# Second chunk of rows through the DMA transposes, six tiles of w1 on the first chunk, scales one by one

## The chip, the cores and the metric

The kernel runs on one core of one Trainium2 chip. The metric is the device time of one execution in microseconds (us), lower is better; a program's time is the median of its runs.

## The reference, cut to what matters

```python
def reference(A_x, A_w_r, A_w_i, B_w1, B_w2):      # x: (1, 2048, 1024), w1: (1024, 3584), w2: (3584, 1024)
    xn = layernorm(A_x)                            # over the last axis, eps 1e-5
    X = rfft2(xn) * (A_w_r + 1j * A_w_i)
    s = irfft2(X)
    g = silu(silu(xn @ B_w1) @ B_w2)
    return A_x + s * g
```

Everything is float32. The two matrix products are the bulk of the arithmetic; the 2-D Fourier filter `s` is made of matrix products with constant matrices and of butterflies.

## The kernel before, in words

The 2048 rows are four chunks `c` of 512 rows, each of four blocks `p` of 128 rows. The 3584 hidden columns are 28 tiles `f` of 128. To keep float32 accuracy every factor is split into two float16 halves, a high one and a low one, and a product takes three passes (high·high, high·low, low·high).

**The first product.** `mm1(c, f)` makes one tile (c, f): 24 matmuls 128x128 by 128x512 into one PSUM tile `pa`. It needs `xnT[c]`, the normalised chunk transposed (both halves, all four blocks), and `w1t[f]`, both halves of w1's tile f. The matmuls are on TensorE (PE in the profile). Which tile follows which is the list `order` in the main loop. After a tile, ScalarE (ACT) evacuates it with a Silu (`evac`, L465) into `h32`. The `pa` tiles and the column sums share four PSUM buffers in rotation.

**w1's tiles.** `weights1` loads a tile `w1r` by the SP queue, takes the maximum of each partition on VectorE (`maxi`, DVE L274), sums it over the partitions with a small matmul (`column_sums`, PE L258), makes a power-of-two scale from that (`scales`, four to six tiny DVE operations, L279 to L287), then the high half on ACT (`split`, L251) and the low half on DVE (`rest`, L254). In the kernel before, scales are made for two tiles at once. Raw tiles and finished tiles share seven buffers.

**Chunks.** `ln_gen(c)` normalises a chunk: `stats` on DVE (two BN_STATS and an aggregate per block), three tiny POOL operations for the scale and shift, the normalisation itself on ACT (`norm`, L700). Chunks 0 and 1 are then transposed on PE (`trans`, eight 128x128 transposes a block), and their halves are taken from PSUM (`hi` on ACT L713, `lo` on DVE L717). Chunks 2 and 3 are in `TURNED`: `turned` normalises into a tile `xp` whose columns are permuted, takes the halves in SBUF (`xs`; high on ACT L678, low on DVE L671), and has the SP queue issue two DMA transposes a block (`turn`, L664). `xp` has two buffers, so the third block's normalisation waits until the first block's low half is done. `xs` has one buffer for all chunks, and it is also the buffer of the Fourier stage's `V`.

**What follows a pair of tiles.** When tiles f and f+1 of chunks 0 and 1 (or 2 and 3) are evacuated, `hidden(q, g)` turns them into seven products' operands: `hr` and a rewrite of `h` on DVE (L494, L495, L499), then `hosum` (from `hr`) and `hoone` (from `h`): a high half on ACT (L251), a low half on DVE (L254), and three or four stores by SP (L488). `hosum` and `hoone` have one buffer each: the next pair's high half waits until the stores of the pair before have landed. `h32` has two buffers.

**What sets the order.** Each engine runs its instructions in the order in which the program issues them and waits at each for its semaphores. The main loop issues a tile of PE work, then steps the generators in the queues `wq` (weights) and `bg` (chunks, then the Fourier stages); for the first four tiles the numbers of steps are written out by hand, later `work` steps them by two counters of issued work. Once built, the order on every engine is fixed. `fa_mat(c, p)` is a block's first Fourier matmuls (24 small ones, L773 to L775), `fa_evac` its two copies on ACT (L782, L783); `FILL` places the first two of chunk 0 between tiles.

Of the kernel before, what the change touches and what calls it, by code (L numbers as in the profile page):

```python
# [23 lines left out]
IORDER = (1, 3, 0, 2)  # L24
SUMMED = (4, 5)
TURNED = (2, 3)
FILL = ((1, 0), (3, 0))
EXTRA = (4, 5, 6, 7, 20, 22, 24)

# [98 lines left out]
def spectral_ffn(ctx, tc, x, w_r, w_i, w1, w2, ca, kc, ci, tw, pm, out):  # L128
# [132 lines left out]
    def weights1():  # L261

        raw = {}

        def load(i):
            raw[i] = fp.tile([128, 8, 128], F32, name=f"w1r{i}", tag="w1", bufs=7)  # L270
            nc.sync.dma_start(raw[i], w1v[:, :, i * 128:(i + 1) * 128])

        def maxi(i):
            nc.vector.tensor_reduce(m1[:, i:i + 1], raw[i], axis=AX.XY, op=OP.max, apply_absolute_value=True)  # L274

        def scales(i, k):
            sl = slice(i, i + k)
            ps = column_sums(f"s1_{i}", m1[:, sl], k)
            nc.vector.tensor_single_scalar(e1[:, sl].bitcast(I32), ps.bitcast(I32), 0x7F800000, op=OP.bitwise_and)  # L279
            nc.vector.tensor_single_scalar(e1[:, sl], e1[:, sl], 2.0**-100, op=OP.max)  # L280
            nc.vector.reciprocal(r1[:, sl], e1[:, sl])
            nc.vector.tensor_single_scalar(rs[:, sl], r1[:, sl], 2.0**14, op=OP.mult)
            nc.gpsimd.tensor_single_scalar(s1[:, sl], e1[:, sl], 2.0**-24, op=OP.mult)
            if (i + k) % 2 == 0:
                p = (i + k) // 2 - 1
                nc.vector.tensor_tensor(ep[:, p:p + 1], e1[:, 2 * p:2 * p + 1], e1[:, 2 * p + 1:2 * p + 2], op=OP.max)
                nc.vector.tensor_tensor(hs[:, p:p + 1], r1[:, 2 * p:2 * p + 1], r1[:, 2 * p + 1:2 * p + 2], op=OP.min)  # L287
                nc.gpsimd.tensor_single_scalar(hs[:, p:p + 1], hs[:, p:p + 1], 2.0**7, op=OP.mult)

        new = {}  # L290

        def split(i):
            new[i] = fp.tile([128, 2, 8, 128], F16, name=f"w1_{i}", tag="w1", bufs=7)
            high(new[i][:, 0], raw[i], rs[:, i:i + 1])

        def rest(i):
            w1t[i] = w = new.pop(i)
            low(w[:, 1], raw.pop(i), rs[:, i:i + 1], w[:, 0])

        for i in range(4):  # L300
            load(i)
        yield 0
        maxi(0)
        yield 0
        maxi(1)
        yield 0
        scales(0, 2)
        yield 0
        split(0)
        yield 0  # L310
        rest(0)
        yield 0
        split(1)
        rest(1)
        maxi(2)
        maxi(3)
        yield 0
        scales(2, 2)
        split(2)
        rest(2)  # L320
        yield 2
        split(3)
        rest(3)
        yield 2
        def ahead(i):

            if i < NFT and i not in raw and i - len(used1) <= 4:
                load(i)
                load(i + 1)

        last = None
        for i in range(4, NFT, 2):
            while i not in raw:
                ahead(i)
                yield 0
                if last is not None:
                    rest(last)
                    last = None
            maxi(i)
            if last is not None:  # L340
                rest(last)
            yield 0
            maxi(i + 1)
            yield 0
# [12 lines left out]
            yield 0.2  # L357
            last = i + 1
        rest(last)
# [89 lines left out]
    def mm1(c, f):  # L449
        ps = pf.tile([128, 512], F32, name=f"pa{c}_{f}", tag="ff")  # L450
        w, xt = w1t[f], xnT[c]
        terms = [(d, wh, xh) for wh, xh in ((0, 0), (0, 1), (1, 0)) for d in range(8)]
        if c + f:
            terms.sort(key=lambda k: k[0])
        for n, (d, wh, xh) in enumerate(terms):
            nc.tensor.matmul(ps, w[:, wh, d], xt[:, xh, d], start=(n == 0), stop=(n == 23))  # L456
        if c == 3:
            used1.add(f)
        q, g = f // 2, c // 2

        def evac():
            if (q, g) not in h32:
                h32[q, g] = H["p"].tile([128, 4, 512], F32, name=f"h32_{q}_{g}", tag="h32", bufs=2)
            hq = h32[q, g]
            nc.scalar.activation(hq[:, 2 * (c % 2) + f % 2], ps, AF.Silu, scale=s1[:, f:f + 1])  # L465
            if c % 2 and f % 2:
                return hidden(q, g)

        return evac
# [187 lines left out]
    def turned(c, stats, norm):  # L657
# [9 lines left out]
        for i in range(4):  # L667
# [15 lines left out]
                    stats(p)  # L683
            yield 2.5

    def ln_gen(c):
        ap = A["p"]

        def stats(p):
            xt = A["x"][c, p]  # L690
            st = ap.tile([128, 2, 6], F32, name=f"st{c}_{p}", tag="st", bufs=4)
            nc.vector.bn_stats(st[:, 0], xt[:, 0:512])
            nc.vector.bn_stats(st[:, 1], xt[:, 512:1024])
            mv = ap.tile([128, 2], F32, name=f"mv{c}_{p}", tag="mv", bufs=4)
            nc.vector.bn_aggr(mv, st.rearrange("p a b -> p (a b)"))
            v = ap.tile([128, 3], F32, name=f"v{c}_{p}", tag="v", bufs=4)
            nc.gpsimd.tensor_scalar(v[:, 0:1], mv[:, 1:2], EPS, 2.0**-20, op0=OP.add, op1=OP.mult)
            nc.gpsimd.tensor_tensor(v[:, 1:2], v[:, 0:1], mhalf, op=OP.pow)
            nc.gpsimd.tensor_scalar(v[:, 2:3], mv[:, 0:1], v[:, 1:2], -1.0, op0=OP.mult, op1=OP.mult)
            norm[p] = lambda o=xt, i=xt: nc.scalar.activation(o, i, AF.Identity, scale=v[:, 1:2], bias=v[:, 2:3])  # L700

        pst, norm = {}, {}

        def trans(p):
            ps = pt.tile([128, 8, 128], F32, name=f"tp{c}_{p}", tag="ft")
            xt = A["x"].pop((c, p))
            xv = xt.rearrange("s (d0 d1) -> s d1 d0", d1=8)
            for d in range(8):
                nc.tensor.transpose(ps[:, d], xv[:, d], ident)
            pst[p] = ps  # L710

        def hi(p):
            nc.scalar.activation(xnT[c][:, 0, :, p * 128:(p + 1) * 128], pst[p], AF.Copy)  # L713

        def lo(p):
            sl = slice(p * 128, (p + 1) * 128)
            nc.vector.tensor_tensor(xnT[c][:, 1, :, sl], pst.pop(p), xnT[c][:, 0, :, sl], op=OP.subtract)  # L717

        new_xnT(c)
        if c == 0:  # L720
            for p in range(2):
                stats(p)
                norm[p]()
            trans(0)
            hi(0)
            stats(2)
            norm[2]()
            trans(1)
            hi(1)
# [12 lines left out]
            lo(3)  # L742
            yield 0
            return
        if c in TURNED:
            yield from turned(c, stats, norm)
            return
        for i in range(4):
            pair = range(2 * (i % 2), 2 * (i % 2) + 2)
            for p in pair:  # L750
                if i < 2:
                    stats(p)
                else:
                    trans(p)
                    if c < 3:
                        load_x(c + 1, p)
            if i < 2:
                yield 2.5
                for p in pair:
                    norm[p]()  # L760
                continue
            for fn in (hi, lo):
                for p in pair:
                    fn(p)
            yield 2.5

    psa, l0 = {}, {}

# [641 lines left out]
    with tc.manual_schedule():  # L1410
# [70 lines left out]
        for c in range(4):  # L1481
            add(bg, fd_gen(c))

        order = [(c, f) for fs in ((0, 1, 2, 3), (4, 5)) for c in range(2) for f in fs]
        order += [(2, 0), (2, 1), (2, 2), (3, 0), (3, 1), (2, 3), (3, 2), (3, 3), (2, 4), (2, 5), (3, 4), (3, 5)]
        order += [(c, f + i) for f in range(6, NFT - LAST, 2) for c in range(4) for i in range(2)]
        order += [(2 * g + c, f + i) for g in range(2) for f in range(NFT - LAST, NFT, 2) for c in range(2) for i in range(2)]
# [2 lines left out]
        for n, (c, f) in enumerate(order):  # L1490
# [32 lines left out]
            if left == 0:  # L1523
                for j, k in ((2, 0), (2, 1), (3, 0)):
                    load_h(0, j, k, nc.sync)
            if n < 4:
                slot(wq)
                for _ in range((2, 0, 1, 1)[f]):
                    slot(bg)
                settle()  # L1530
                fresh_ev[0] = ev
                tick()
                continue
# [81 lines left out]
```

## Time and profile before

| | us |
|---|---|
| median of 3 runs (1239.05 to 1243.32) | 1241.05 |
| the profiled execution's own time | 1238.48 |
| its span (first to last instruction) | 1236.6 |
| PE busy, of the span | 1221.4 |
| DVE busy | 998.6 |
| ACT busy | 467.3 |
| DMA, mean | 237 GB/s |

PE, DVE, ACT and POOL are the four compute engines, PEld is PE's weight load, SP the engine that issues most transfers ("SPq" in the timeline is its queue). In a timeline a row has the start in us, the duration, the engine, the line and the operation, the tiles (out<-in) and, in brackets, the idle time before it and what ended that. Rows merge equal instructions that follow each other ("x24").

### The profile page before, as it was taken

How to read it: one execution, taken by the hardware profiler on the slowest of the kernel's cores; microseconds unless marked ns; L12 is line 12 of the kernel's file. 1: busy time of each engine (PE TensorE's matmuls, PEld its weight loads, DVE VectorE, ACT ScalarE, POOL GpSimd, SP SyncE). 2: the span in 40 equal slices, each digit the busy share in tenths (PEclk: the TensorE clock that was granted, in tenths of full speed). 3: DMA queues.
4: the chain of work that ended last, by engine and by line, in shares of the span. 5: the costliest groups of instructions: out<-in, count | busy, mean ns of one | idle time of the engine just before them, and what ended most of it. 6: DMA issues, size and time to landing. Idle time of an engine off the chain costs nothing.

```text
span 1236.6 us, 19106 instructions
## 1 busy us (share of the span) xinstructions
PE 1221.4 (99%) x7033; PEld 624.6 (51%) x7033; DVE 998.6 (81%) x1970; ACT 467.3 (38%) x614; POOL 117.3 (9%) x245
## 2 busy tenths in 40 slices
PE   8999999999999999999999999999999999999997
PEld 5545445444544454445445555554455555555544
DVE  7687988899798898886959899985196678798885
ACT  4865344333454565344533222122032222342212
POOL 2330000001000000010001121114111110000000
PEclk9999999999999999999999999999999999999999
DMA  8487476655768898759899999987979999997677
GB/s 251 136 171 186 134 224 204 186 147 166 218 178 237 283 280 242 213 178 272 206 287 223 281 256 200 303 251 238 294 206 275 293 287 320 319 348 292 223 261 231
DMA packets 271102, 293.67 MB, mean 237 GB/s; under 512 B 40096, under 2 KB 198816, under 8 KB 270624
## 3 DMA queue, kind: packets, MB, share of 16 engines
q1 hardware_dynamic: 250992, 233.66, 65.4%
q10 hardware_dynamic: 15984, 51.45, 12.0%
q0 software_dynamic: 4032, 7.34, 3.4%
q8 instruction: 55, 0.90, 0.3%
q14 instruction: 39, 0.32, 0.1%
HBM read 185.95 MB, written 102.25 MB: 233 GB/s over the span
## 4 chain that ended last, share of the span: by engine, by line
PE 87%; DMA 6%; DVE 4%; ACT 1%; issue 1%; SPq 0%; POOL 0%; ACTq 0%; DVEq 0%; POOLq 0%
PE pa L456 45%; PE pb L534 11%; PE pb L536 11%; PE pb L535 11%; DMA out_dram<-pl 2%; PE fx L945 2%; PE id L1285 1%; DMA sd<-s 1%; PE fx L947 1%; PE iu L1195 1%; PE fx L946 1%; ACT xp L700 1%; PE iu L1203 1%; DMA pl<-pd 1%; DMA fs<-sd 1%
## 5 line engine op out<-in xcount | busy, mean ns | idle before, releaser
L456 PE MATMUL pa<-xnT,w 128*128 128x512 f16 x2688 | 585.2, 379 | 1.1 <-ACT w L251 0.7
L456 PEld LDWEIGHTS <-w 128*128 128x128 f16 x2688 | 261.7, 98 | 312.1 <-DVE w L254 1.3
L534 PE MATMUL pb<-w,ht 128*128 128x512 f16 (+2 forms) x812 | 300.6, 372 | 0.0
L535 PE MATMUL pb<-w,ht 128*128 128x512 f16 (+2 forms) x812 | 300.6, 372 | 0.0
L536 PE MATMUL pb<-w,ht 128*128 128x512 f16 (+2 forms) x812 | 300.6, 372 | 0.0
L536 PEld LDWEIGHTS <-ht 128*128 128x128 f16 x812 | 79.3, 98 | 91.2
L534 PEld LDWEIGHTS <-ht 128*128 128x128 f16 x812 | 79.4, 98 | 86.8
L535 PEld LDWEIGHTS <-ht 128*128 128x128 f16 x812 | 79.3, 98 | 86.8
L465 ACT ACTIVATE h<-pa,s 128x512 f32<-128x512 f32 x112 | 75.5, 678 | 120.9 <-PE pa L456 108.9
L251 ACT ACTIVATE w<-jr,sc 128x512 f16<-128x512 f32 x98 | 68.1, 713 | 78.3 <-DMA jr<-in_B_w_dram 39.4
L254 DVE SCALAR_TENSOR_TENSOR hoone<-h,hs,hoone 128x2048 f16<-128x2048 f32 x28 | 65.7, 2345 | 8.9 <-ACT hoone L251 8.9
L254 DVE SCALAR_TENSOR_TENSOR w<-jr,sc,w 128x512 f16<-128x512 f32 x98 | 71.0, 743 | 2.1 <-ACT w L251 2.1
L251 ACT ACTIVATE hoone<-h,hs 128x2048 f16<-128x2048 f32 x28 | 56.0, 1998 | 38.5 <-DVE h L499 25.1
L251 ACT ACTIVATE hosum<-hr,hs 128x1536 f16<-128x1536 f32 x28 | 44.1, 1574 | 65.2 <-DVE hr L495 31.7
L972 ACT ACTIVATE zq<-Z,zs 128x1024 f16<-128x1024 f32 x16 | 18.4, 1149 | 107.6 <-DVE Z L1046 60.8
L254 DVE SCALAR_TENSOR_TENSOR hosum<-hr,hs,hosum 128x1536 f16<-128x1536 f32 x28 | 50.7, 1812 | 3.8 <-ACT hosum L251 3.8
L494 DVE TENSOR_TENSOR hr<-h 128x1024 f32<-128x1024 f32 x28 | 34.2, 1221 | 23.2 <-ACT h L465 23.1
L251 ACT ACTIVATE w<-w1r,rs 128x1024 f16<-128x1024 f32 x28 | 32.0, 1145 | 46.6 <-DVE w L254 31.4
L274 DVE TENSOR_REDUCE m<-w1r 128x1 f32<-128x1024 f32 x28 | 33.8, 1211 | 17.9 <-DMA w1r<-in_B_w_dram 17.9
L622 ACT ACTIVATE pl<-pl,c 128x512 f32<-128x512 f32 (+2 forms) x28 | 17.6, 657 | 72.3 <-DVE pl L601 33.9
L945 PE MATMUL fx<-vq,kq 128*128 128x256 f16 x192 | 43.2, 273 | 0.0
L946 PE MATMUL fx<-vq,kq 128*128 128x128 f16 x192 | 42.1, 219 | 0.0
(219 smaller groups left out, 1526.2 us busy)
## 6 DMA issues: line engine op xcount, KB each, us to landing
w1r<-in_B_w_dram SPq DMA_DIRECT2D x28, 512.0 KB, 6.3
hd_sum<-hosum SPq DMA_DIRECT2D x56, 256.0 KB, 2.9
hd_one<-hoone SPq DMA_DIRECT2D x56, 256.0 KB, 3.6
hd_dif<-hoone SPq DMA_DIRECT2D x56, 256.0 KB, 3.2
w2m<-in_B_w_dram SPq DMA_DIRECT2D x28, 512.0 KB, 5.2
ht<-hd_dif ACTq DMA_DIRECT2D x32, 448.0 KB, 6.0
jr<-in_B_w_dram SPq DMA_DIRECT2D x56, 256.0 KB, 6.8
ht<-hd_sum ACTq DMA_DIRECT2D x32, 448.0 KB, 5.5
```

What stands on the lines that cost most here:

```text
L251: nc.scalar.activation(hi, raw, AF.Copy, scale=scale)
L254: nc.vector.scalar_tensor_tensor(lo, raw, scale, hi, op0=OP.mult, op1=OP.subtract)
L274: nc.vector.tensor_reduce(m1[:, i:i + 1], raw[i], axis=AX.XY, op=OP.max, apply_absolute_value=True)
L456: nc.tensor.matmul(ps, w[:, wh, d], xt[:, xh, d], start=(n == 0), stop=(n == 23))
L465: nc.scalar.activation(hq[:, 2 * (c % 2) + f % 2], ps, AF.Silu, scale=s1[:, f:f + 1])
L494: tt(sums[:, 0:2], hq[:, 0::2], hq[:, 1::2], op=OP.subtract)
L534: nc.tensor.matmul(ps, hh[:, 0], w[:, 0], start=first, stop=False)
L535: nc.tensor.matmul(ps, hh[:, 0], w[:, 1], start=False, stop=False)
L536: nc.tensor.matmul(ps, hh[:, 1], w[:, 0], start=False, stop=last)
L945: nc.tensor.matmul(o, k[:, c, kh, 1], v[:, c, vh], start=(n == 0), stop=False)
L946: nc.tensor.matmul(ps[:, c, 0], k[:, c, kh, 2], v[:, c, vh, 128:256], start=False, stop=False)
L972: nc.scalar.activation(zqs[q][:, 0, :, 16 * j:16 * j + 16], zs_[u], AF.Copy, scale=zs)
```

## The change

Chunk 1 no longer takes the path over PE: it goes through a new generator `entering`, which normalises, splits and DMA-transposes block by block. So that PE has work meanwhile, the list `order` begins with the six tiles (0,0) to (0,5), then (1,0) to (1,5), where it was (0,0) to (0,3), (1,0) to (1,3), (0,4), (0,5), (1,4), (1,5). For that, tiles 4 and 5 of w1 are loaded and split early, and the scales of tiles 2 to 5 are made one by one, each column sum between two tiles. The string `ENTRY` gives the generators' steps behind the first five tiles ("b" a step of the chunks, "w" a step of the weights). Chunk 0's results of tiles 4 and 5 go to a spare tile `h32_early` and are copied into `h32` later. `FILL` puts chunk 0's first two Fourier blocks ahead of (0,4) and (1,0).

```diff
-FILL = ((1, 0), (3, 0))
-EXTRA = (4, 5, 6, 7, 20, 22, 24)
+FILL = ((0, 4), (1, 0))
+EXTRA = (20, 22, 24)
+ENTRY = ("bwbw", "bwbwb", "wbwbw", "wbwbw", "b")
...
     # weights1
         split(1)
+        yield 0
         rest(1)
+        load(4)
         maxi(2)
+        yield 0
+        scales(2, 1)
+        split(2)
+        load(5)
         maxi(3)
-        yield 0
-        scales(2, 2)
-        split(2)
         rest(2)
-        yield 2
+        yield 0
+        scales(3, 1)
+        maxi(4)
         split(3)
+        yield 0
         rest(3)
-        yield 2
+        yield 0
+        scales(4, 1)
+        yield 0
+        split(4)
+        yield 0
+        rest(4)
+        maxi(5)
+        yield 0
+        scales(5, 1)
+        yield 0
+        split(5)
+        yield 0
+        rest(5)
+        yield 0
...
-        for i in range(4, NFT, 2):
+        for i in range(6, NFT, 2):
...
     # mm1
-        if c + f:
+        if f or c > 1:
             terms.sort(key=lambda k: k[0])
...
         def evac():
+            if (q, c) == (2, 0):
+                if f % 2 == 0:
+                    h32["early"] = A["p"].tile([128, 2, 512], F32, name="h32_early", tag="Ro", bufs=1)
+                nc.scalar.activation(h32["early"][:, f % 2], ps, AF.Silu, scale=s1[:, f:f + 1])
+                return None
             if (q, g) not in h32:
                 h32[q, g] = H["p"].tile([128, 4, 512], F32, name=f"h32_{q}_{g}", tag="h32", bufs=2)
+                if (q, c) == (2, 1):
+                    nc.scalar.activation(h32[q, g][:, 0:2], h32.pop("early"), AF.Copy)
...
+    def entering(c, stats, norm):
+        ap = A["p"]
+        split = ap.tile([128, 4, 2, 8, 128], F16, name=f"xs{c}", tag="V", bufs=1)
+        xn = {}
+        def plain(p):
+            xn[p] = ap.tile([128, 8, 128], F32, name=f"xp{c}_{p}", tag="Rs", bufs=2)
+            norm[p](xn[p].rearrange("s d1 d0 -> s d0 d1"), A["x"][c, p].rearrange("s (d0 d1) -> s d0 d1", d1=8))
+            A["x"].pop((c, p))
+            defer(1, lambda: load_x(c + 1, p))
+        def hi(p):
+            nc.scalar.activation(split[:, p, 0], xn[p], AF.Copy)
+        def turn(p, h):
+            nc.sync.dma_start_transpose(
+                xnT[c][:, h, :, p * 128:(p + 1) * 128], split[:, p, h].rearrange("s d1 d0 -> s (d1 d0)"))
+        def lo(p):
+            turn(p, 0)
+            nc.vector.tensor_tensor(split[:, p, 1], xn.pop(p), split[:, p, 0], op=OP.subtract)
+            turn(p, 1)
...
     # ln_gen: the path of chunk 1 over PE goes
-        if c in TURNED:
-            yield from turned(c, stats, norm)
-            return
-        for i in range(4):
...
+        yield from (turned if c in TURNED else entering)(c, stats, norm)
...
     # main loop
-        order = [(c, f) for fs in ((0, 1, 2, 3), (4, 5)) for c in range(2) for f in fs]
+        order = [(c, f) for c in range(2) for f in range(6)]
...
-            if n < 4:
-                slot(wq)
-                for _ in range((2, 0, 1, 1)[f]):
-                    slot(bg)
+            if n < len(ENTRY):
+                for k in ENTRY[n]:
+                    slot(wq if k == "w" else bg)
```

From w1's tile 26 on every engine's instructions stand in the same order as before; on PE that holds from tile 22. Two places where the order differs are shown. Names are those of the program: `xp3_2` is the normalised block 2 of chunk 3, `xs3` its halves, `hosum_0_1_0` and `hoone_0_1_0` the operands of pair q = 1 (tiles 2 and 3), `h32_2_0` and `hr2_0` those of pair 2 (tiles 4 and 5), `pa1_5` the PSUM tile (1,5).

DVE, where chunk 3's low halves are made, in the kernel before:

```order
L254 SCALAR_TENSOR_TENSOR hosum_0_1_0_978<-hr1_0_946,hs_227,hosum_0_1_0_978 128x12x128
L671 TENSOR_TENSOR xs3_897<-xp3_0_987,xs3_897 128x1024
L671 TENSOR_TENSOR xs3_897<-xp3_1_990,xs3_897 128x1024
L254 SCALAR_TENSOR_TENSOR hoone_0_1_0_1036<-h32_1_0_669,hs_227,hoone_0_1_0_1036 128x16x128
L671 TENSOR_TENSOR xs3_897<-xp3_2_1049,xs3_897 128x1024
L671 TENSOR_TENSOR xs3_897<-xp3_3_1052,xs3_897 128x1024
L494 TENSOR_TENSOR hr2_0_1118<-h32_2_0_981 128x1024
L495 TENSOR_TENSOR hr2_0_1118<-h32_2_0_981 128x512
```

The same place on DVE in the changed kernel (its own line numbers):

```order
L255 SCALAR_TENSOR_TENSOR hosum_0_1_0_1075<-hr1_0_1019,hs_227,hosum_0_1_0_1075 128x12x128
L521 TENSOR_TENSOR hr2_0_1114<-h32_2_0_1078 128x1024
L522 TENSOR_TENSOR hr2_0_1114<-h32_2_0_1078 128x512
L698 TENSOR_TENSOR xs3_971<-xp3_0_1025,xs3_971 128x1024
L698 TENSOR_TENSOR xs3_971<-xp3_1_1028,xs3_971 128x1024
L255 SCALAR_TENSOR_TENSOR hoone_0_1_0_1110<-h32_1_0_672,hs_227,hoone_0_1_0_1110 128x16x128
L526 TENSOR_TENSOR h32_2_0_1078<-h32_2_0_1078 128x2x512
L698 TENSOR_TENSOR xs3_971<-xp3_2_1126,xs3_971 128x1024
L698 TENSOR_TENSOR xs3_971<-xp3_3_1129,xs3_971 128x1024
```

The two `hr2_0` operations, which read the whole `h32_2_0`, have moved ahead of all four low halves of chunk 3.

ACT, where chunk 3's normalisations stand, in the changed kernel:

```order
L252 ACTIVATE hosum_0_1_0_1075<-hr1_0_1019,hs_227 128x12x128
L490 ACTIVATE h32_2_0_1078<-h32_early_759 128x1024
L492 ACTIVATE h32_2_0_1078<-pa1_4_990,s1_225 128x512
L252 ACTIVATE hoone_0_1_0_1110<-h32_1_0_672,hs_227 128x16x128
L492 ACTIVATE h32_2_0_1078<-pa1_5_1049,s1_225 128x512
L778 ACTIVATE xp3_2_1126<-x3_2_931,v3_2_1036 128x128x8
L705 ACTIVATE xs3_971<-xp3_2_1126 128x1024
L778 ACTIVATE xp3_3_1129<-x3_3_933,v3_3_1045 128x128x8
L705 ACTIVATE xs3_971<-xp3_3_1129 128x1024
```

The same place on ACT in the kernel before:

```order
L700 ACTIVATE xp3_1_990<-x3_1_799,v3_1_912 128x128x8
L678 ACTIVATE xs3_897<-xp3_1_990 128x1024
L251 ACTIVATE hoone_0_1_0_1036<-h32_1_0_669,hs_227 128x16x128
L465 ACTIVATE h32_2_0_981<-pa0_5_952,s1_225 128x512
L700 ACTIVATE xp3_2_1049<-x3_2_852,v3_2_998 128x128x8
L678 ACTIVATE xs3_897<-xp3_2_1049 128x1024
L700 ACTIVATE xp3_3_1052<-x3_3_854,v3_3_1007 128x128x8
L678 ACTIVATE xs3_897<-xp3_3_1052 128x1024
L465 ACTIVATE h32_2_0_981<-pa1_4_1011,s1_225 128x512
```

In both, `hoone_0_1_0` and one evacuation stand ahead of blocks 2 and 3 of chunk 3; in the changed kernel the evacuation is the one that completes `h32_2_0`, and `hosum_0_1_0` has moved behind blocks 0 and 1 of chunk 3.

More of the change, by code (lines that the diff above doesn't have):

```diff
@@ L313, in weights1 @@
         split(1)
+        yield 0
         rest(1)
+        load(4)
         maxi(2)
+        yield 0
+        scales(2, 1)
+        split(2)
+        load(5)
         maxi(3)
+        rest(2)
         yield 0
-        scales(2, 2)
-        split(2)
-        rest(2)
-        yield 2
+        scales(3, 1)
+        maxi(4)
         split(3)
+        yield 0
         rest(3)
-        yield 2
+        yield 0
[12 more added lines that the diff above has]
+        yield 0
         def ahead(i):
@@ L684, in turned @@
             yield 2.5
+    def entering(c, stats, norm):
[16 more added lines that the diff above has]
+            turn(p, 1)
+        stats(0)
+        yield 0
+        plain(0)
+        hi(0)
+        stats(1)
+        yield 0
+        lo(0)
+        plain(1)
+        hi(1)
+        yield 0
+        stats(2)
+        yield 0
+        stats(3)
+        yield 0
+        lo(1)
+        plain(2)
+        yield 0
+        hi(2)
+        yield 0
+        lo(2)
+        plain(3)
+        yield 0
+        hi(3)
+        yield 0
+        lo(3)
+        yield 0
     def ln_gen(c):
@@ L744, in ln_gen @@
             return
-        if c in TURNED:
-            yield from turned(c, stats, norm)
-            return
-        for i in range(4):
[L749 to L765, printed above, removed]
+        yield from (turned if c in TURNED else entering)(c, stats, norm)
     psa, l0 = {}, {}
```

## The prediction

> **What bounds the kernel now.** I read the page first, then the busy times by stage, then the waits of PE.
>
> ```profile
> span 1236.6 us, 19106 instructions
> ...
> PE 1221.4 (99%) x7033; PEld 624.6 (51%) x7033; DVE 998.6 (81%) x1970; ACT 467.3 (38%) x614; POOL 117.3 (9%) x245
> ...
> 140.00:400.00 260.00, 260.00 (x1356) 124.61 (x1355) 224.30 (x445) 114.23 (x128) 12.68 (x23) 1.00 0.66 193
> 700.00:820.00 120.00, 120.00 (x766) 65.78 (x764) 113.31 (x211) 27.35 (x38) 20.39 (x38) 1.00 0.97 247
> ```
>
> The last two rows are stages: their length, then busy PE, PEld, DVE, ACT and POOL, then clock and DMA. PE is busy for the whole of both. So PE bounds the kernel, and a microsecond of PE taken away or added before 140 us should reach the end whole. The change lies before 140 us. There the rows of PE are these (the first two from the chain that ended last, the others from PE's timeline):
>
> ```profile
> 24.79 0.12 PE s L258 x2
> ...
> 35.28 1.78 PE tp L709 x16
> ...
> 42.08 1.95 PE L709 MATMUL tp<-ident,x 128*128 128x128 f32 x16
> 45.50 0.22 PE L773 MATMUL fa<-cas,xnT 128*128 128x128 f16 x1 [1.47 <-DVE xnT L717]
> ...
> 68.68 30.90 PE L456 MATMUL pa<-xnT,w 128*128 128x512 f16 x142 [0.40 <-DVE w L254]
> 99.42 0.22 PE L773 MATMUL fa<-cas,xnT 128*128 128x128 f16 x1
> ...
> 107.28 5.34 PE L456 MATMUL pa<-xnT,w 128*128 128x512 f16 x24
> ```
>
> The 142 matmuls from 68.68 to 99.42 give 0.2165 us each, so a tile of 24 takes 5.19 us. A Fourier block `fa` takes 1.33 us (99.42 to the next tile at 100.75). The tile at 107.28 is (3,0), the first of chunk 3.
>
> **What the change takes from PE.** Chunk 1's 32 transposes: 1.78 us for the first 16 and, 1.95 less what overlaps the tile before, 1.79 us for the others, 3.57 in all. The wait of 1.47 us behind them goes too: it is `fa`'s wait for a PSUM buffer that chunk 1's `lo` still read, and no such `lo` is left. The 0.40 us for w1's tile 4 goes, since tile 4 is split earlier. Sum: −5.44 us. Moving Fourier blocks between tiles moves no PE work away; their number is the same.
>
> **What it adds on PE at the entry.** Two more column sums at 0.12 us: +0.24. And waits: with a sum between every two tiles PE now depends on DVE's pace. DVE's durations at the entry:
>
> ```profile
> 19.41 2.48 DVE L254 SCALAR_TENSOR_TENSOR w<-w1r,rs,w 128x1024 f16<-128x1024 f32 x2
> 21.81 2.33 DVE L274 TENSOR_REDUCE m<-w1r 128x1 f32<-128x1024 f32 x2
> ...
> 24.94 0.16 DVE L279 TENSOR_SCALAR e<-s 128x2 int32<-128x2 int32 x1 [0.80 <-PE s L258]
> ...
> 25.69 0.15 DVE L287 TENSOR_TENSOR hs<-r 128x1 f32<-128x1 f32 x1
> ```
>
> In the new order DVE has, between 19.41 and the maximum of tile 5, five low halves of w1 (1.20), four maxima (1.17), four blocks' `stats` (1.49, from rows below), three `scales` (0.8, less for the short ones) and two low halves of chunk 1 (1.14): 6.0 + 4.7 + 6.0 + 2.2 + 2.3 = 21.2, with short waits for ACT about 21.6, so it ends near 41.0. PE has four tiles and three sums from 19.43 on, so it asks at 40.6. I take +0.5 for this wait; 0 to 2 are the bounds, since a late low half can hold a tile as well. Chunk 1 itself is then ready in time: its last low half ends near 46, its last DMA transpose lands by 52.6 (5.9 us at worst, below), and PE comes to (1,0) at 40.6 + 0.5 + 0.12 + 2 × 1.33 + 2 × 5.19, about 54.3. The eight added DMA transposes wait in SP's queue with the loads of chunk 2's rows between them; those have until 55, and before they were issued from 36 to 55 anyway. POOL's tiny operations only move. ACT pays more for chunk 1 (a permuting normalisation takes 2.17 us, in the next rows), hidden behind PE's six tiles.
>
> **What is late next: chunk 3.** After (1,0) PE has nine tiles to (3,0): 54.3 + 9 × 5.19 = 101.0, against 107.28 before. Is chunk 3 there? I follow the queues from the last Fourier block (ends 54.5) with these rows of ACT, then of DVE, SP and the transfers:
>
> ```profile
> 47.04 0.61 ACT L782 ACTIVATE L<-fa 128x520 f32<-128x520 f32 x1 [1.35 <-PE fa L775]
> 48.01 0.69 ACT L465 ACTIVATE h<-pa,s 128x512 f32<-128x512 f32 x1
> 49.47 2.17 ACT L700 ACTIVATE xp<-x,v 128x1024 f32<-128x1024 f32 x1 [0.77 <-POOL v L699]
> ...
> 62.63 0.67 ACT L465 ACTIVATE h<-pa,s 128x512 f32<-128x512 f32 x1
> ...
> 80.19 1.58 ACT L251 ACTIVATE hosum<-hr,hs 128x1536 f16<-128x1536 f32 x1 [5.88 <-DMA hd_sum_d<-hosum]
> ...
> 88.56 1.99 ACT L251 ACTIVATE hoone<-h,hs 128x2048 f16<-128x2048 f32 x1
> 90.45 0.67 ACT L465 ACTIVATE h<-pa,s 128x512 f32<-128x512 f32 x1
> ```
>
> ```profile
> 63.34 1.23 DVE L494 TENSOR_TENSOR hr<-h 128x1024 f32<-128x1024 f32 x1 [4.93 <-ACT h L465]
> ...
> 65.08 2.35 DVE L671 TENSOR_TENSOR xs<-xp,xs 128x1024 f16<-128x1024 f32 x2
> 67.35 1.27 DVE L254 SCALAR_TENSOR_TENSOR w<-w1r,rs,w 128x1024 f16<-128x1024 f32 x1
> 68.55 1.22 DVE L499 TENSOR_TENSOR h<-h 128x1024 f32<-128x1024 f32 x1
> 69.68 0.68 DVE L692 BATCH_NORM_STATS2 st<-x 128x6 f32<-128x512 f32 x1
> ...
> 72.65 1.23 DVE L254 SCALAR_TENSOR_TENSOR w<-w1r,rs,w 128x1024 f16<-128x1024 f32 x1
> 73.80 1.81 DVE L254 SCALAR_TENSOR_TENSOR hosum<-hr,hs,hosum 128x1536 f16<-128x1536 f32 x1
> 75.71 1.23 DVE L494 TENSOR_TENSOR hr<-h 128x1024 f32<-128x1024 f32 x1
> ...
> 77.46 2.34 DVE L254 SCALAR_TENSOR_TENSOR hoone<-h,hs,hoone 128x2048 f16<-128x2048 f32 x1
> ```
>
> ```profile
> 81.81 0.66 SPq L488 DMA_DIRECT2D hd_one<-hoone  x1
> ...
> 94.43 0.54 SPq L488 DMA_DIRECT2D hd_one<-hoone  x1
> ...
> 97.45 5.98 SPq L664 DMA_TRANSPOSE xnT<-xs  x4
> ...
> hd_one<-hoone SPq DMA_DIRECT2D x2, 256.0 KB, 3.0
> ...
> DMA to landing us min/median/max: 3.1/4.0/5.9
> ```
>
> (The last two rows: time from issue to landing, median for a store of `hoone`, and the extremes for the transposes.)
>
> 1. ACT: two copies of the Fourier block (0.97), an evacuation (0.57 to 0.69), four normalisations with their high halves and an evacuation between (49.47 to 62.63, 13.16), then the evacuation of (1,1) (0.7): 54.5 + 15.4 = 69.9. Before, that evacuation ended at 63.3.
> 2. DVE then has `hr` (1.74), two low halves (2.27), the rewrite of `h` (1.13), two `stats` (2.97), the low `hosum` (1.91), `hr` of the next pair (1.75), two `stats` (3.0), the low `hoone` (2.34): 17.1, so 87.0. Before, it was 79.8; two `stats` are now ahead of `hoone`.
> 3. SP stores `hoone` in four pieces. Before, the low half ended at 79.8, the last piece was issued at 81.81 and landed 3.0 later, 5.0 in all: now 92.1.
> 4. ACT stands for that at `hoone` of pair 1, which needs the one buffer; the row at 80.19 shows such a wait. Queued behind it are the evacuation of (1,5) and blocks 2 and 3 of chunk 3. The high `hoone` takes 1.9, the evacuation 0.7: 94.7. Before, ACT came to `hoone` only at 88.56 and waited for nothing.
> 5. DVE stands at `hr2_0` for that evacuation; behind it are all low halves of chunk 3. `hr` 1.75, blocks 0 and 1 2.3, low `hoone` 2.3: 101.1, which frees the next stores; block 2's normalisation starts at 97.8, since its buffer is block 0's.
> 6. SP: three transposes to about 102, four stores (94.43 to about 97.0 before, 2.6), then four transposes. From 97.45 to the landing of the last, issued at 102.1, were 7.4 to 8 us. So the last lands near 104.6 + 7.7 = 112.3.
>
> PE stands at (3,0), whose first two matmuls read all eight transposes, from 101.0 to about 112.4: **+11.4 us**. The bounds are 8 (every transfer at its least, short pieces on DVE) and 14. Chunk 2 has no such trouble: it ends 79 to 81, needed at 85.5. Behind (3,0) the order of work catches up: when DVE has finished pair 2 and its first Fourier block, near 117, PE is where it was at about 111 before, so I see no second wait.
>
> **The clock.** PE's idle gaps in the trace are at most 1.5 us, and the table of stages shows a granted clock of 1.00. What PE does after a long idle is seen only at the start:
>
> ```profile
> 0.99 6.82 PE L1456 MATMUL spin<-ones 128*128 128x256 f16 x35 [0.99 <-POOL mhalf L1470]
> ...
> 17.25 1.47 PE L1456 MATMUL spin<-ones 128*128 128x256 f16 x12
> ```
>
> At the later pace 35 would take 4.3; the first ones lost 2.5. The price of restarting after 11 us lies between 0 (the 1.47 us gap, after which matmuls ran at their usual pace) and 2.5. I take 2.0, nearer to the start, since 11 us is long. The Trainium skill, "TensorE: Matmul & The Clock Gate", "HAM oscillation", states that an idle gap over some 3.4 us drops the array to half clock; with its warm-up window of 3.4 us an estimate by that page is a loss of 1.7 us or more. By it the sum would be about the same, and a shorter chunk 3 wait of 4 us would cost the clock as well; no gap in this trace is long enough to show it.
>
> **Sum.** −5.44 + 0.24 + 0.5 + 11.4 + 2.0 = +8.7 us. Cross-check without the clock: (3,0) at 112.4 with one more Fourier block (1.33) still to come, against 107.28, is +6.45; the terms give +6.7. The profiled execution took 1238.48, so 1247.2 for such a one; the median of the runs is 2.6 above it, 1241.05, so **1249.7** for a median.
>
> **The rivals.** *Chunk 3 in time.* If its last transpose lands by 101.0, only the saving is left: −5.44 + 0.24 + 0.5 = −4.7, and 1236.3. For it: before, the same transposes landed by about 105.2, 2 us ahead of (3,0), so the chain was tight but held, and three of its waits are for transfers. Against it: it must be 11.4 us shorter than the rows make it. It decides at that point. Chance 0.11. *Half of it.* Steps 2 to 6 are some 5 to 7 us shorter than summed, PE waits 5 us, too short for much loss of clock: −4.7 + 5 = +0.3, 1241.3. Chance 0.08. *The entry fails too.* The scales one by one leave PE no slack (41.0 against 40.6); if DVE or ACT run 1 us late at each of four tiles, that is +4 on top of the forecast, 1253.7. ACT's queue is in favour: its normalisations stand between the weights' high halves. Against: the low halves of tiles 2 and 3 have 0.3 to 0.8 us to spare by the same sum. Chance 0.15. *Chunk 1 late as well,* if its transposes land after 54.3, has 2 us to spare and is counted there. That the change doesn't remove the transposes can't be: PE's order has only chunk 0's left.
>
> **How the numbers follow.** The forecast has 0.66: 1244 (wait of 8, no clock) to 1253 (14, clock 2.5). With the entry's case the range is 1243 to 1256, 0.81 of the chance. A measurement of this kernel tells about 0.3% (3.7 us) from no change. Faster by that: the first rival, 0.11. Same: the second and the forecast's lower edge, 0.09. Slower: 0.80.
>
> **What would show it.** In the changed profile: no `tp` of chunk 1; waits at the entry under 2 us; ACT idle some 3.5 us before the second `hoone`, ended by a store; DVE idle before `hr` at about 90 to 95; and one wait of PE of about 11 us, before the tile that follows (2,2), ended by a DMA transpose. Without that wait I am wrong, and the time is about 1236.

## The result, and the profile after

The changed kernel takes 1251.39 us (median of 6 runs, 1248.57 to 1255.46); the kernel before took 1242.41 in the same comparison. The ratio is 1.0066, with a 95% interval from 1.0043 to 1.0088. Measured once more beside the last experiment it is 1.0094 (1.0073 to 1.0115), 1252.62 against 1240.84. So the change costs some 9 to 12 us. The forecast was 1249.7 in 1243 to 1256.

| profiled execution, us | before | after |
|---|---|---|
| its own time | 1238.48 | 1250.69 |
| span | 1236.6 | 1248.9 |
| PE busy | 1221.4 | 1220.1 |
| PE's wait for chunk 3's transposes | none | 12.0 |

First the page of the changed kernel, then PE's waits ahead of 160 us (waited for; us in total, times, longest), then PE's timeline around the wait:

```profile
span 1248.9 us, 19085 instructions
PE 1220.1 (98%) x7005; PEld 622.3 (50%) x7005; DVE 999.7 (80%) x1978; ACT 472.0 (38%) x615; POOL 118.1 (9%) x247
PEclk9997999999999999999999999999999999999999
```

```profile
PE pa L476 <- DMA xnT<-xs: 12.0, 2, 11.3
...
PE s L259 <- DVE m L275: 1.6, 1, 1.6
```

```profile
42.07 0.38 PE L259 MATMUL s<-m,ones 128*128 128x1 f32 x2 [1.63 <-DVE m L275]
...
55.35 46.78 PE L476 MATMUL pa<-xnT,w 128*128 128x512 f16 x216
113.44 0.59 PE L476 MATMUL pa<-xnT,w 128*128 128x512 f16 x1 [11.31 <-DMA xnT<-xs]
114.68 7.88 PE L476 MATMUL pa<-xnT,w 128*128 128x512 f16 x23 [0.65 <-DMA xnT<-xs]
122.40 0.22 PE L831 MATMUL fa<-cas,xnT 128*128 128x128 f16 x1
...
123.74 10.52 PE L476 MATMUL pa<-xnT,w 128*128 128x512 f16 x48
```

PE runs nine tiles without a gap (216 matmuls to 102.1), stands for chunk 3's DMA transposes at (3,0), does one matmul, stands 0.65 more, and then takes 7.72 us (114.68 to 122.40) for 23 matmuls, where 23 × 0.2165 = 4.98 is usual. It reaches the tile behind at 123.74; the kernel before was there at 107.28 + 5.19 = 112.47. That is 11.3 us behind. The clock of that stretch, in the busy times by stage (length, PE, PEld, DVE, ACT, POOL, clock, DMA share, GB/s):

```profile
101.00:115.00 14.00, 2.04 (x8) 0.53 (x6) 10.64 (x9) 10.45 (x9) 0.00 (x0) 0.70 1.03 225
115.00:140.00 25.00, 25.00 (x141) 12.25 (x140) 14.76 (x50) 6.62 (x7) 0.22 (x2) 0.89 0.39 105
```

The first stage is mostly the wait itself. Cut finer, the granted clock is 0.50 in every slice from 107 to 120 us and 1.00 again from 121 us: PE runs at half clock for the first 5.6 us of the 23 matmuls.

The chain that leads there, in the timelines of ACT, DVE and SP:

```profile
70.24 0.67 ACT L492 ACTIVATE h<-pa,s 128x512 f32<-128x512 f32 x1
...
94.11 2.00 ACT L252 ACTIVATE hoone<-h,hs 128x2048 f16<-128x2048 f32 x1 [4.51 <-DMA hd_one<-hoone]
96.02 0.67 ACT L492 ACTIVATE h<-pa,s 128x512 f32<-128x512 f32 x1
99.78 2.19 ACT L778 ACTIVATE xp<-x,v 128x1024 f32<-128x1024 f32 x1 [3.09 <-DVE xs L698]
```

```profile
85.64 2.30 DVE L255 SCALAR_TENSOR_TENSOR hoone<-h,hs,hoone 128x2048 f16<-128x2048 f32 x1
...
96.72 1.23 DVE L521 TENSOR_TENSOR hr<-h 128x1024 f32<-128x1024 f32 x1 [5.92 <-ACT h L492]
...
100.74 2.34 DVE L255 SCALAR_TENSOR_TENSOR hoone<-h,hs,hoone 128x2048 f16<-128x2048 f32 x1
```

```profile
89.95 0.67 SPq L515 DMA_DIRECT2D hd_one<-hoone  x1
...
93.36 10.35 SPq L691 DMA_TRANSPOSE xnT<-xs  x4
...
106.55 6.17 SPq L691 DMA_TRANSPOSE xnT<-xs  x4
```

ACT waits 4.51 us for the store of pair 0's `hoone` and only then makes the eviction (1,5) (96.02). DVE waits 5.92 us for that eviction, with all of chunk 3's low halves behind it. ACT in turn waits 3.09 us for the first low half, since that frees the buffer for block 2's normalisation. SP's first four transposes are stretched over 10.35 us by the missing halves.

### The profile page after: what moved, and what is told of

Read it like the earlier page. It is cut to its first block, busy times and chain, and to the rows that moved or that the text cites. A ratio compares the mean times of both kernels' runs of the same rounds, so it can differ in the third digit from the quotient of the medians.

```text
span 1248.9 us, 19085 instructions
## 1 busy us (share of the span) xinstructions
PE 1220.1 (98%) x7005; PEld 622.3 (50%) x7005; DVE 999.7 (80%) x1978; ACT 472.0 (38%) x615; POOL 118.1 (9%) x247
## 4 chain that ended last, share of the span: by engine, by line
PE 83%; DVE 7%; DMA 5%; ACT 3%; issue 1%; SPq 1%; POOL 0%; ACTq 0%; DVEq 0%; POOLq 0%
PE pa L476 41%; PE pb L563 11%; PE pb L561 11%; PE pb L562 11%; DMA out_dram<-pl 3%; PE fx L1003 2%; ACT xp L778 1%; PE id L1343 1%; PE iu L1253 1%; PE fx L1005 1%; PE fx L1004 1%; PE iu L1261 1%; DMA sd<-s 1%; PE fa L831 1%; PE fa L833 1%
```

## The experiments

The theory is the prediction's chain: store of pair 0's `hoone`, ACT's `hoone` of pair 1, eviction (1,5), DVE's `hr2`, chunk 3's low halves, its transposes. The rival is that the four blocks of chunk 1 now sent through DMA transposes on SP make chunk 3's late by their traffic or their place in the queue. These are eight transposes, two a block; the expectations below speak of four. All edits are made to the changed kernel.

**Chunk 3's halves ahead of the pairs' work.** One more step of the chunks' generator behind the tiles n = 10 and n = 11 of `order`:

```diff
             after(ev)
+            if n in (10, 11):
+                slot(bg)
```

> The changed kernel, with chunk 3's preparation moved two tiles earlier in the order: all four normalisations, low halves and both groups of transposes of chunk 3 stand ahead of the row-pair work of pair 1 and of the wait for hr2 on ACT, DVE and SP. Nothing is left out. If the wait at (3,0) comes from that chain (store of pair 0's operands, hoone of pair 1 on ACT, eviction (1,5), hr2 on DVE, then chunk 3's low halves), the wait of 11.3 us is under 1 us, the clock stays at full rate there, and the profiled time is 1236 to 1240 us, 11 to 14 us below the changed kernel's 1250.7: the 5.4 us taken off TensorE come through, less 1.6 us of the wait at the entry. If the four added DMA transposes of chunk 1 and their traffic are what makes chunk 3 late, the order matters little: 8 us or more of the wait stay and the time is 1247 us or more.

Measured: 1239.12 us (12 runs) against 1241.92, ratio 0.9975 (0.9959 to 0.9991). DVE and PE:

```profile
86.54 2.36 DVE L698 TENSOR_TENSOR xs<-xp,xs 128x1024 f16<-128x1024 f32 x2
...
95.68 1.23 DVE L698 TENSOR_TENSOR xs<-xp,xs 128x1024 f16<-128x1024 f32 x1 [2.25 <-ACT xs L705]
...
101.31 1.23 DVE L521 TENSOR_TENSOR hr<-h 128x1024 f32<-128x1024 f32 x1 [2.34 <-ACT h L492]
```

```profile
98.68 10.52 PE L476 MATMUL pa<-xnT,w 128*128 128x512 f16 x48 [1.07 <-ACT h L492]
```

All low halves are done at 96.9, ahead of `hr`, and PE goes through (2,2) and (3,0) in one row of 48 matmuls; its only wait is 1.07 us for a PSUM buffer, since ACT now makes two normalisations ahead of an eviction. The same transposes of chunk 1 are there. So order, not the added transposes, made the 12 us. With the order mended the change is worth its saving, 5.2 us less 1.6 at the entry and 1.07 here, which is 2.5; the median is 2.8 us below the kernel before, and 12 below the changed kernel.

**One tile earlier only.** The same with `if n == 11`.

> The changed kernel, with chunk 3's preparation moved one tile earlier only: on DVE the low halves of blocks 0 and 1 now stand ahead of hr2, those of blocks 2 and 3 still behind it, and the last four transposes still behind the stores of pair 1's operands. Nothing is left out. By the chain, the first transposes are early but the last still hang on DVE's wait for hr2 at about 98 us plus two low halves and a group of transposes: the wait at (3,0) shrinks to 3 to 8 us but does not go, and the time is 1242 to 1248 us. By the added DMA transposes as the cause: 8 us or more stay, 1247 us or more.

Measured: 1251.90 us, ratio 1.0073 (1.0050 to 1.0096), the wait 10.9 + 0.7 us where I expected 3 to 8. PE, then ACT, then DVE:

```profile
112.97 0.58 PE L476 MATMUL pa<-xnT,w 128*128 128x512 f16 x1 [10.86 <-DMA xnT<-xs]
```

```profile
93.50 2.14 ACT L778 ACTIVATE xp<-x,v 128x1024 f32<-128x1024 f32 x1
...
96.64 1.99 ACT L252 ACTIVATE hoone<-h,hs 128x2048 f16<-128x2048 f32 x1
98.53 0.67 ACT L492 ACTIVATE h<-pa,s 128x512 f32<-128x512 f32 x1
```

```profile
99.23 1.23 DVE L521 TENSOR_TENSOR hr<-h 128x1024 f32<-128x1024 f32 x1 [6.15 <-ACT h L492]
...
104.37 2.35 DVE L698 TENSOR_TENSOR xs<-xp,xs 128x1024 f16<-128x1024 f32 x2
```

The normalisations of blocks 2 and 3 now fill the time in which ACT had waited for the store, so `hoone` comes 2.5 us later instead of earlier and the eviction with it. DVE reaches `hr` later, and the last two low halves still stand behind it. A wait on ACT was filled, but the same instruction on DVE still held the last halves back: half a reordering moved nothing.

**PE kept busy during the wait.**

```diff
+            if (c, f) == (3, 0):
+                spin(100)
             ev = mm1(c, f)
```

> The changed kernel, with 100 matmuls whose result nobody reads (128x256, about 11 us of TensorE) put ahead of (3,0), where TensorE stood idle. Nothing is left out. The transposes of chunk 3 land when they did (about 113.4 us), so (3,0) starts when it did. If the slow 23 matmuls behind the wait (7.7 us where 5.0 us is full rate) are the price of the idle gap, they take about 5.0 us and the profiled time falls by 2 to 3 us, to 1247.5 to 1249 us. If the low clock has another cause, the time stays within 0.5 us of 1250.7.

```profile
102.18 11.08 PE L1514 MATMUL spin<-ones 128*128 128x256 f16 x100
114.41 0.38 PE L476 MATMUL pa<-xnT,w 128*128 128x512 f16 x1 [1.15 <-DMA xnT<-xs]
115.60 5.14 PE L476 MATMUL pa<-xnT,w 128*128 128x512 f16 x23 [0.81 <-DMA xnT<-xs]
```

The 23 matmuls take 5.14 us instead of 7.88, so the 2.7 us are the price of the idle gap, and no slice of the page's clock is under 0.9. The transposes landed 1.0 us later here, so PE is 1.8 us ahead of the changed kernel at the tile behind (121.91 against 123.74) and 2.8 at its last matmul. The profiled time fell by 1.4 only (1249.31, just above the expected 1247.5 to 1249), because the work behind PE's last matmul took 11.0 us here and 9.6 there. The median is 1249.49, ratio 1.0066 (1.0040 to 1.0091). By time alone it can't be told from the changed kernel.

**Chunk 1 transposed on PE, in the new order of tiles.** Each block's eight transposes and its halves from PSUM as in the kernel before; the DMA transposes of chunk 1 go.

```diff
-        yield from (turned if c in TURNED else entering)(c, stats, norm)
+        if c in TURNED:
+            yield from turned(c, stats, norm)
+        else:
+            yield from entering(c, stats, norm, trans, hi, lo)
```

> The changed kernel's order of w1 tiles and scales, but chunk 1 is transposed on TensorE as in the kernel before (32 transposes, 3.6 us by the prediction's row), so that the four added DMA transposes on SP are gone. Nothing is left out. By the chain, which starts at the end of chunk 1's transposition and runs over ACT and DVE, chunk 3 is as late as before relative to TensorE: a wait of 9 to 12 us stays at (3,0), and the time is 1252 to 1256 us, the transposes coming on top. If the added DMA transposes are what makes chunk 3 late, the wait falls to 2 us or less and the time is 1240 to 1244 us.

```profile
61.56 46.78 PE L476 MATMUL pa<-xnT,w 128*128 128x512 f16 x216
119.14 0.58 PE L476 MATMUL pa<-xnT,w 128*128 128x512 f16 x1 [10.79 <-DMA xnT<-xs]
120.26 7.62 PE L476 MATMUL pa<-xnT,w 128*128 128x512 f16 x23 [0.54 <-DMA xnT<-xs]
```

The wait stays, 11.3 us, though none of the added transposes is left. The rival is out. PE comes to the nine tiles at 61.56 instead of 55.35, and the time is 1257.69 us, ratio 1.0121 (1.0098 to 1.0145), 1.7 above the expected 1252 to 1256. That expectation left out PE's waits around the transposes: 1.1 us for DVE behind them, and 4.6 us in all for ACT's normalised blocks where the changed kernel has 2.9.

The same entry with chunk 3 early, as in the first experiment:

> The kernel of e1_lows_early with chunk 1 transposed on TensorE as in e4_chunk1_on_PE: chunk 3 is in time, and the only thing left to compare with e1_lows_early is the entry. Nothing is left out. By the prediction's terms the transposes cost TensorE 3.6 us, and 1 to 2.5 us of waits for ACT and DVE behind them, against 1.6 us of wait that the entry by DMA has: the time is 3 to 6 us above e1_lows_early, 1242 to 1245 us, equal to or slower than the kernel before. If the DMA transposes save nothing (the entry is bound by DVE either way), it is within 1 us of e1_lows_early.

Measured 1244.95 us, ratio 1.0031 (1.0014 to 1.0049), 5.8 us above the first experiment's median, as expected. So with chunk 3 in time the path by DMA is the better one for chunk 1, and the new order of tiles with transposes on PE is some 4 us slower than the kernel before.

**The entry wait.** DVE's maximum of tile 5 stood behind the low half of tile 4, which itself waited for ACT; in the first experiment's timeline:

```profile
40.27 1.28 DVE L255 SCALAR_TENSOR_TENSOR w<-w1r,rs,w 128x1024 f16<-128x1024 f32 x1 [0.99 <-ACT w L252]
```

On top of that experiment, the two change places:

```diff
-        rest(4)
         maxi(5)
+        rest(4)
```

> The kernel of e1_lows_early, with the maximum of w1's tile 5 on DVE swapped to stand ahead of the low half of tile 4. Nothing is left out. If the 1.6 us that TensorE waits for the column sum of tile 5 are only DVE's order (the maximum stood behind a low half that itself waited 1.0 us for ACT), the wait goes under 0.3 us, the low half of tile 4 comes just in time for (0,4), and the profiled time falls by 1.3 to 1.7 us against e1_lows_early, to about 1236.5 by medians. If DVE is simply overloaded at the entry, the wait moves to (0,4) or (0,5) and the time stays within 0.5 us of e1_lows_early's.

```profile
40.38 0.28 PE L259 MATMUL s<-m,ones 128*128 128x1 f32 x2
```

The column sum follows its tile without a wait. The median is 1237.96 us, ratio 0.9972 (0.9954 to 0.9989): the lowest here, some 3 us below the kernel before. Against the first experiment the traces show the wait gone; the times, 1.2 us apart by medians (1.3 to 1.7 expected) and 0.03% by ratios, can't tell them apart.

**The links one by one.** First the store: pair 0's `hoone` isn't stored, so ACT waits for nothing at pair 1's.

```diff
             def rest():
                 low(ov[1], sv, sc, ov[0])
+                if (q, g, n) == (0, 0, 4):
+                    return
...
```

> The changed kernel without the stores of pair 0's hoone (pair 2's is stored in its place as well, so pair 0's share of four products is left out); ACT then has nothing to wait for at hoone of pair 1. If the wait of 4.5 us there is a link of the chain, eviction (1,5), hr2, chunk 3's low halves and its last transposes all come about 4 us earlier: the wait at (3,0) falls from 12.0 in all to 7 to 9 us and the time to 1246 to 1248 us. If chunk 3 is late for another reason (transfers, or DVE's amount of work), the wait stays at 11 to 12 us.

Then DVE's `hr2`, issued one step later:

```diff
-                return hidden(q, g)
+                return (lambda: hidden(q, g)) if (q, g) == (2, 0) else hidden(q, g)
```

> The changed kernel with hr2 issued one step later, so that on DVE it stands behind the low halves of blocks 0 and 1 of chunk 3 and the low hoone of pair 1 (blocks 2 and 3 still behind it); ACT's order up to there is the same and it still waits for the store. Nothing is left out. If DVE standing at hr2 is a link, the normalisations of blocks 2 and 3 start about 3 us earlier and the last low half ends near 104 instead of 107.5: the wait at (3,0) falls from 12.0 to 8 to 9.5 us, the time to 1247 to 1249 us. If only ACT's wait for the store counts, the wait stays at 11 to 12 us.

The first of these rows is the store's experiment, the second that of `hr2`:

```profile
109.01 0.61 PE L476 MATMUL pa<-xnT,w 128*128 128x512 f16 x1 [6.64 <-DMA xnT<-xs]
```

```profile
109.42 0.59 PE L476 MATMUL pa<-xnT,w 128*128 128x512 f16 x1 [7.23 <-DMA xnT<-xs]
```

In all, PE waits 7.4 and 7.8 us instead of 12.0. Without the store the eviction (1,5) starts at 91.63 instead of 96.02 and the last low half ends at 103.1 instead of 107.5. With `hr2` late ACT still waits 4.51 us, but block 2's normalisation starts at 96.65 instead of 99.78 and the last low half ends at 104.4. So both links are real; each taken away alone shortens the wait by 4.2 to 4.6 us. Both together:

> The edits of e6_no_store_wait and e7_hr_late together (pair 0's share of four products is left out). ACT's wait for the store and DVE's wait for hr2 are both gone. If the two links add up, the wait at (3,0) falls by 4.6 and 4.2 us, from 12.0 to about 3 us. But in the traces of e6 and e7 SP issues without a break: stores of hosum to 93.4, four transposes of 6.2 us, four stores of hoone of 2.6 us, four transposes of 6.2 us, to 108.7. If that queue is the link behind both, nothing more is gained: the wait stays at 7 to 8 us, and the time at 1245 to 1248 us.

The wait is 7.5 us: nothing more is gained, although DVE has the last low half at 99.9 instead of 107.5. SP in this run:

```profile
90.93 1.20 SPq L521 DMA_DIRECT2D hd_sum<-hosum  x2
92.17 0.67 SPq L521 DMA_DIRECT2D hd_sum_d<-hosum  x1
92.88 6.19 SPq L697 DMA_TRANSPOSE xnT<-xs  x4
99.17 0.54 SPq L521 DMA_DIRECT2D hd_one<-hoone  x1
99.75 1.36 SPq L521 DMA_DIRECT2D hd_dif<-hoone  x2
101.16 0.71 SPq L521 DMA_DIRECT2D hd_one<-hoone  x1
101.97 6.38 SPq L697 DMA_TRANSPOSE xnT<-xs  x4
```

SP issues without a break from 90.9 to 108.4. Below the chain lies a second bound, some 4 us shorter, which the prediction didn't price by itself. It holds already in the two single experiments, where SP issues as densely up to 108.3 and 108.7, so a link alone may be worth more than it shows there. Is it the order in SP's queue? Pair 1's stores issued by POOL instead:

```diff
+                eng = nc.gpsimd if (q, g) == (1, 0) else nc.sync
-                    defer(1, lambda k=k, m=m: nc.sync.dma_start(
+                    defer(1, lambda k=k, m=m: eng.dma_start(
```

> The kernel of e9_both_links (pair 0's share of four products is left out), with the seven stores of pair 1's operands issued by POOL's queue instead of SP's, so that chunk 3's transposes have nothing between them on SP. If SP's queue is the link that e9 leaves, the first four transposes go out from about 90.7 and the last four as soon as their halves are made (about 99.8): the last lands near 104 to 106, the wait at (3,0) is 2 to 4 us and the time 1241 to 1244 us. If the transposes' own transfers are the limit, the wait stays at 6 us or more.

It isn't only that: the wait is 8.0 us (7.6 + 0.4), the time 1251.08 us, ratio 1.0077 (1.0049 to 1.0106). PE's wait (the profile names no releaser for it), one transpose in SP's timeline, and two of the stores of `hoone` in the list of DMA issues (KB each, median us to landing):

```profile
110.02 0.58 PE L476 MATMUL pa<-xnT,w 128*128 128x512 f16 x1 [7.61 <-issue]
```

```profile
99.30 5.06 SPq L698 DMA_TRANSPOSE xnT<-xs  x1
```

```profile
hd_one<-hoone POOLq DMA_DIRECT2D x2, 256.0 KB, 7.3
```

With nothing between them on SP, single transposes take up to 5.06 us to issue (1.2 to 1.9 in the run before), and POOL's stores of `hoone` land after 7 to 8 us instead of 3 to 4. I read this as the transfers themselves in each other's way between 91 and 109 us. The busy share of the 16 DMA engines speaks for it where SP's queue stays in order: 0.92 from 91 to 99 us and 1.0 from there to 108.4. With POOL's stores it is 0.70 from 91 to 99 us and full only behind that, though transposes are slow to issue there too (2.3 and 2.8 us). So POOL's own path for stores may add to it, and no run separates the two.

**Do the microseconds reach the end?** The two experiments on single links cut PE's wait by over 4 us, but their medians (1249.41 us, ratio 1.0059, 1.0035 to 1.0084, above the expected 1246 to 1248; and 1248.52, 1.0060, 1.0041 to 1.0079) fell less. Both together gave 1246.86 (1.0053, 1.0034 to 1.0073). So the changed kernel and that with `hr2` late ran side by side once more:

> The changed kernel itself once more, beside the kernel of e7_hr_late, to see whether microseconds of the wait at (3,0) reach the time whole. If they do, the wait at (3,0) is again 11 to 12.5 us, and the ratio to the kernel before is 1.007 to 1.010: by the traces TensorE ends 10.2 us behind.

> The kernel of e7_hr_late once more, beside the changed kernel. In e7's trace the wait at (3,0) was 4.2 us shorter and (3,0)'s Fourier block done 4.3 us sooner, but the medians of the two calls differ by 0.06% only. If the 4.3 us reach the end, the medians of this call are 3.5 to 5 us apart. If later waits (for the Fourier stage or for the second product's transfers) take it back, they are under 2 us apart and such waits show in the trace behind 160 us.

The changed kernel: 1252.62 us, wait 12.0, ratio 1.0094 (1.0073 to 1.0115). With `hr2` late: 1249.59, wait 7.9, ratio 1.0069 (1.0046 to 1.0092). The medians are 3.0 us apart, of the 4.1 us in the wait. PE's waits behind 160 us, first of the changed kernel, then with `hr2` late:

```profile
PE iu L1261 <- DVE ub L1270: 3.0, 1, 3.0
```

```profile
PE iu L1261 <- DVE ub L1270: 2.2, 1, 2.2
PE pb L561 <- DMA ht<-hd_dif: 2.1, 1, 2.1
PE eps L1136 <- POOL edge L1130: 0.2, 1, 0.2
```

4.5 against 3.0 us: 1.5 us are given back at the Fourier stage and at the second product's transfers. The trace with `hr2` late loses over 2 us more that no wait shows: PE is 3.4 us ahead at the tile behind (3,0) and 0.6 us behind at its last matmul. Most of it is the clock. From 855.7 to 859.1 us it runs at 0.50, behind the Fourier stage's small matmuls `eps`, and eight matmuls start 0.43 us apart instead of 0.22: 1.7 us. Of the other traces three have such a spell between 160 us and PE's last matmul, that of the store's experiment among them, and neither trace of the changed kernel has one. And what follows PE's last matmul takes 6.8 to 11.0 us over all traces here. So a microsecond won at (3,0) can be lost again, and single executions can't be compared to better than some 4 us.

## Why the prediction was right

**The saving** came as summed, but for the entry. **The entry wait** was 1.63 us, not 0.5, inside the bounds of 0 to 2. The term that was mis-sized is DVE's "short waits for ACT", taken as 0.4 us in all. In the changed kernel DVE waited for ACT 1.06 us ahead of the low half of tile 3 and 0.98 us ahead of that of tile 4 (0.99 in the first experiment's row above), 2.0 in all; putting the maximum ahead of the latter removed the whole wait.

**The six steps** held, with what they inherit: the entry's extra 1.1 us shifts PE's arrival too (101.0 predicted, 102.1 measured).

| step | predicted | measured |
|---|---|---|
| 1: eviction (1,1) ends | 69.9 | 70.9 |
| 2: low `hoone` of pair 0 ends | 87.0 | 87.9 |
| 3: its stores have landed | 92.1 | 94.1 |
| 4: eviction (1,5) ends | 94.7 | 96.7 |
| 5: low `hoone` of pair 1 ends | 101.1 | 103.1 |
| 6: PE goes on at (3,0) | 112.4 | 113.4, then 114.7 |

Step 3 lost 1 us more than summed (the last piece went out at 89.95 and landed 4.2 us later, not 3.0), and PE waited a second time, 0.65 us, for a last transpose. The wait came to 11.96 us against 11.4. The prediction named ACT's and DVE's waits as they stand in the trace, and taking either away shortens the wait, so the chain is shown and not only argued. What it lacked is what the experiment with both links gone showed: at 7 to 8 us a second bound takes over. The bounds of 8 to 14 were made from the chain; the near one happens to lie where the other bound begins. With a chain 5 to 7 us shorter, as the rival "Half of it" supposed, that bound would still have kept the wait at 7 to 8 us, not 5: with both links gone the last low half comes 7.6 us earlier and PE still waits 7.5.

**The clock** cost 2.74 us against 2.0 assumed, just over its bound of 2.5. The second trace of the changed kernel has it cheaper behind the same wait:

```profile
114.75 6.51 PE L476 MATMUL pa<-xnT,w 128*128 128x512 f16 x23 [0.52 <-DMA xnT<-xs]
```

Against 5.14 the 23 matmuls lost 1.4 to 2.9 us behind waits of 10.8 to 11.4 us (four traces) and 1.65 to 2.5 us behind waits of 6.6 to 7.6 us (five). The loss is half of the time until the full clock is back: 5.6 us from their start in the first trace of the changed kernel, 2.8 in the second. So it varies between executions more than with the length of the wait, and my scale "nearer to the start, since 11 us is long" has no support here; the rival "Half of it" took 5 us as too short for much loss, and no run has a wait that short there. That a gap of this length drops the clock is what the Trainium skill, "TensorE: Matmul & The Clock Gate", "HAM oscillation", states: the traces agree, with 0.50 granted from within the gap on. Its estimated loss of 1.7 us or more fits seven of the nine traces; 1.65 and 1.4 lie under it. The gap of 3.4 us isn't the only way, though: the spell at `eps` above came behind a wait of 0.2 us. (The prediction's "at most 1.5 us" for gaps in the trace of before overlooked one of 1.83 us near 1063 us; the clock stayed at 1.00 behind it.)

**The sum.** With the measured sizes, −5.44 + 0.24 + 1.63 + 11.96 + 2.74 = +11.1; PE is 11.3 us behind at the tile after (3,0). From there it is 10.2 us behind at its last matmul (before, then after):

```profile
1228.86 0.22 PE L536 MATMUL pb<-w,ht 128*128 128x128 f16 x1
```

```profile
1239.07 0.22 PE L563 MATMUL pb<-w,ht 128*128 128x128 f16 x1
```

The forecast sum, 8.7, was 2.6 us short by the trace. The profiled executions are even 12.2 us apart: PE's 10.2, and 2.1 more behind its last matmul (9.6 us there instead of 7.5), a stretch that the change doesn't touch. The forecast of the median is closer than that, 1.7 us, and this is luck: the profiled execution of before was a quick one of its kernel (2.6 us under the median used, 3.9 under the later one), that of after only 0.7 under its own, and some 1 us of the delay is given back ahead of the last matmul. The sign and the mechanism were derived; the last two microseconds of agreement were not.

## What to carry to other kernels

When a change moves work earlier on the bounding engine, ask what that engine reaches next and follow the queues of the other engines to it: here 3.6 us saved at the entry (5.44 less 0.24 and 1.63) brought a 12 us wait two chunks later, because the work for eight transposes stood behind an instruction that waited for someone else's store. In queues that keep their order, first look for an instruction on the consumer's path that stands behind a wait it doesn't need; move all of its followers, since moving half of them can give nothing. And when removing two waits together brings no more than either alone, the next bound is below both: look at the transfers and their queue.

## What the runs showed of the hardware

After an idle gap of PE of 6.6 to 11.4 us, 23 matmuls took 6.5 to 8.0 us instead of 5.0, and matmuls with no use in the gap kept full pace (5.14). In four of these traces cut finely the granted clock fell to 0.50 between 3.4 and 5.1 us into the gap and came back to 1.00 between 2.8 and 5.6 us after the start of the 23 matmuls, in no order of the gap's length. A spell of half clock came without such a gap too: 24 matmuls took 6.63 us instead of 5.34 behind a wait of 1.78 us and eight transposes (chunk 1 on PE with chunk 3 early), and not behind the same wait of 1.76 us in the run with chunk 1 on PE alone.

Four DMA transposes took SP about 6.2 us to issue even when their data was ready, and a single one up to 5.06 us while POOL's stores of 256 KB were on their way. The stores of `hoone` landed after 7 to 8 us from POOL's queue and after 3 to 4 from SP's.
